# Sums of weight blocks taken in quarters, probabilities scaled by ScalarE in late chunks, and the first odd weight tiles in the ring

## The chip, the cores and the metric

The kernel runs on one core of a Trainium2 chip. A core has a matrix engine (TensorE, in the profile PE, with its weight loads as PEld), a vector engine (VectorE, DVE), a scalar engine (ScalarE, ACT), GpSimd (POOL) and SyncE (SP), which here only issues transfers; ACT issues transfers too. Each of these engines works through its own list of instructions in order and waits for the others by semaphores. SBUF is the working memory, 128 partitions wide; PE writes its sums to PSUM, from where ACT or DVE take them.

The metric is the device time of one execution in microseconds, as the median of several runs. A profile is one further execution, recorded by the hardware.

## The reference

Two layers in one launch: attention with a band and a few global columns, and after it a feed-forward layer on its output.

```python
batch, n_heads, seq, head_dim = (4, 8, 768, 64);  n_global, n_local = (8, 96)
scores = scale * np.matmul(q, k.transpose(0, 1, 3, 2)) + bias     # bias: -slope of the head * distance
scores = np.where(is_global | is_local, scores, -1e9)
a = np.exp(scores - max); a = a / (np.sum(a, axis=-1, keepdims=True) + 1e-09)
attn = np.matmul(a, v)
x = attn.transpose(0, 2, 1, 3).reshape(3072, 512)                 # 3072 tokens
h = x @ w_in                                                      # 512 -> 2048
out = np.maximum(0.01 * h, h) @ w_out                             # 2048 -> 512
```

All arithmetic stands for float32, and the weights arrive as 64-bit floats. The kernel keeps each factor of a product as a high part, rounded to the matrix engine's format (`fp32r`), and a low part, the rest; a product is three matmuls (high by high, low by high, high by low).

## The kernel before, in words

**Tokens.** The 3072 tokens are 24 steps of 128 (`NSTEP`), put together into 11 chunks of 3, 3 and nine times 2 steps (`CHUNKS`). The feed-forward layer has 16 blocks `f` of 128 hidden columns (`NF`), or 8 pairs `p` of two blocks (`NP`); in a pair, `e` is the even and `o` the odd block.

**Attention.** Each step has two units of four heads, 48 in all. `event(t)` does a slice of three units at once: probabilities by values for unit t−2 (`attn_v`, PE), scores for unit t (`scores`, PE), and for unit t then, on DVE, four bias sums with their minimum (`biased`, L215), on ACT four exponentials with their sums (`exps`, L228), and `sums`: two small DVE instructions give the reciprocal `rs` (L249, L250). From unit 14 on (`BY_DVE`) four DVE instructions then multiply the probabilities by it (L256), one DVE instruction transposes them in blocks (L259), and `move` sends them through DRAM into the layout that `attn_v` needs: one transfer out and four back, on SP. The output of `attn_v` is copied by ACT (`keep_x`, L339) and split into high and low by POOL.

**The first two chunks** go through the ordinary loops `ffn1` and `ffn2` (up to about 203 us), while the weights are converted and kept in SBUF: `wout` whole, `win` as 16 tiles. The eight odd tiles of `win` lie in pool `odd` and are also written to DRAM (`wd`), for that pool is given up afterwards.

**The stage of pairs** takes the other nine chunks, 8 pairs each, as 72 steps `s` (`NS`). In a step, in the order of the source:

- the attention events that are due (`ev_pair`): four to a chunk, in its steps 0, 1, 3 and 5;
- `hidden_pair(s)`: 24 matmuls of 256 columns (L478) give the two hidden blocks of a pair, into a PSUM tile `ps_h` in even steps and into the first half of `bank[0]` (`ps_p`) in odd ones. The odd block's weights come by `fetch` from DRAM into a ring of two tiles, two steps ahead, on ACT's queue (L466);
- `gates(s)`: ACT copies the block to `t` (L489), DVE applies the leaky rectifier (L492) and, for a pair by seven products, four small sums of gate blocks (L495); ACT rounds to `gh` (L499), DVE takes the rest `gl` (L500);
- `out_pair(s - 2)`: the matmuls of two steps earlier into the output banks (L527). An ordinary pair takes 12 matmuls of 512 columns, a pair by seven products (a two by two block product with seven block products) 21 of 256. The second half of the tile `bank[0]` is an output bank. `SEVEN` says, chunk by chunk, how many of the eight pairs go by seven products: the last ones, and in the chunk these come last. At a chunk's end `results` gathers the banks into rows in pool `ev` (three buffers) and sends them out;
- in some steps `prepare(p)`: for seven products, `wout` of a pair needs four sums of blocks, each again as high and low. It is done once per pair, as one burst: 12 DVE sums (L508) and 4 ACT casts (L584), with three buffers of `ev` as scratch. There are seven bursts, in steps 10, 12, 14, 18, 20, 26 and 28. The last of the four sums overwrites a block of `wout` that the ordinary form of the pair needs, so it comes only when the pair's ordinary outputs are done.

**The order of the work.** PE's order is that of the source throughout. The other engines' order is that of the source (`pin`) only up to the middle of the second loop; in the stage of pairs a planner sets it before the run: it goes through the source with estimated durations, and each engine takes, of what is ready by these estimates, what stands first in the source. On the chip the engines then keep that order, whatever the real durations are.

**Memory.** Pools are stacked. At step 1, `later.close()` gives up `ffn`, `kept_rows`, `x0` and `odd`, and the pools `ring`, `a` (`gh`, `gl`), `ev` and `w` (the sums `h`, `l`) take the room. A new pool waits for all use of each old pool that it lies over. `a` lies over `kept_rows`, which holds the last output rows of chunk 0 until they are sent (L434, L442). For this reason `gates(0)` and `gates(1)` both stand behind `hidden_pair(1)`.

Of the kernel before, what the change touches and what calls it, by code (L numbers as in the profile page):

```python
# [18 lines left out]
P = 128  # L19
# [12 lines left out]
PAIR = 2  # L32
SEVEN = [0, 3, 5] + [7] * 6
RING = 2
# [18 lines left out]
def fast_path(ctx, tc, qp, kp, vp, wi, wo, nvec, nmall, out, B, H, S):  # L53
# [12 lines left out]
    keep = ctx.enter_context(tc.tile_pool(name="weights", bufs=1))  # L66
    wout = keep.tile([P, NF, 2, DM], F32R, name="wout")
    win = {f: keep.tile([P, 2, NK, P], F32R, tag=f"win{f}", name="win") for f in range(0, NF, 2)}

    const = ctx.enter_context(tc.tile_pool(name="const", bufs=1))  # L70
# [4 lines left out]
    kept_rows = later.enter_context(tc.tile_pool(name="kept_rows", bufs=1))  # L75
    xts = {0: later.enter_context(tc.tile_pool(name="x0", bufs=1))}
    odd = later.enter_context(tc.tile_pool(name="odd", bufs=1))
    nc.gpsimd.memset(odd.tile([P, 16], F32, tag="gap", name="gap"), 0.0)
    win.update({f: odd.tile([P, 2, NK, P], F32R, tag=f"win{f}", name="win") for f in range(1, NF, 2)})
    wd = ctx.enter_context(tc.tile_pool(name="wd", bufs=1, space=bass.MemoryType.DRAM)).tile(  # L80
# [164 lines left out]
    def sums(u):  # L245
        d = units[u]
        sm = d.pop("sm")
        rs = att.tile([P, 16], F32, name="rs")[:, :4]
        pin(nc.vector.tensor_scalar(out=rs, in0=sm, scalar1=1e-9, scalar2=None, op0=ALU.add))  # L249
        pin(nc.vector.reciprocal(out=rs, in_=rs))  # L250
        if u >= BY_DVE:
            pr = d.pop("pr")
            for a in range(2):
                for j in range(2):
                    p, n = head(u, pr, a, j), 2 * a + j
                    pin(nc.vector.tensor_scalar(out=p, in0=p, scalar1=rs[:, n:n + 1], scalar2=1.0, op0=ALU.mult,  # L256
                                                op1=ALU.mult))
            p = blocks(u, pr).rearrange("p c j x -> p (c j x)")
            pin(nc.vector.transpose(out=p, in_=p))  # L259
            move(u, pr)  # L260
            return

        dg = kept_rows.tile([P, 4, HALF], F32, name="dg")
        pin(nc.gpsimd.tensor_tensor(out=dg, in0=eye.unsqueeze(1).to_broadcast([P, 4, HALF]),
                                    in1=rs.unsqueeze(2).to_broadcast([P, 4, HALF]), op=ALU.mult))
        d["dg"] = dg

    def warm(times):
# [191 lines left out]
    def fetch(s):  # L460

        if s >= NS:
            return
        p = at(s)[1]
        streamed[s] = late["ring"].tile([P, 2, NK, P], F32R, name="ring")
        nc.scalar.dma_start(out=streamed[s].rearrange("p a k x -> p (a k x)").bitcast(F32), in_=wd[p])  # L466
# [14 lines left out]

    def gates(s):

        c, p = at(s)
        ps = pair[s]
        n = 8 if fast(c, p) else 4
        t = late["t"].tile([P, 8, P], F32, name="t")
        g = t[:, :4].rearrange("p a b -> p (a b)")
        pin(nc.scalar.copy(out=g, in_=ps))  # L489
        if s >= RING:  # L490
            fetch(s + RING)
        pin(nc.vector.scalar_tensor_tensor(out=g, in0=g, scalar=0.01, in1=g, op0=ALU.mult, op1=ALU.max))  # L492
        if n == 8:
            for o, x, y, op in ((4, 2, 0, ALU.add), (6, 1, 0, ALU.subtract), (5, 4, 1, ALU.subtract), (7, 3, 5, ALU.subtract)):
                pin(nc.vector.tensor_tensor(out=t[:, o], in0=t[:, x], in1=t[:, y], op=op))  # L495
        a0 = n // 8
        gh = late["a"].tile([P, 7, P], F32R, name="gh")
        gl = late["a"].tile([P, 7, P], F32R, name="gl")
        pin(nc.scalar.copy(out=gh[:, :n - a0], in_=t[:, a0:n]))  # L499
        pin(nc.vector.tensor_tensor(out=gl[:, :n - a0], in0=t[:, a0:n], in1=gh[:, :n - a0].bitcast(F32), op=ALU.subtract))  # L500
        pair[s] = gh, gl, a0

# [66 lines left out]

    def prepare(p):  # L570

        e, o = 2 * p, 2 * p + 1
        first = p == NP - 1
        h = late["w"].tile([P, (4 if first else 3) * GT], F32R, tag=f"h{p}", name=f"h{p}")
        l = late["w"].tile([P, 3 * GT], F32R, tag=f"l{p}", name=f"l{p}")
        sides[p] = h, l
        x = [y[:, n] for y in (late["ev"].tile([P, 2, GT], F32, tag="ev", name="wk") for _ in range(3)) for n in range(2)]

        def whole(to, f, n):
            bh, bl = block(f, n)  # L580
            add(to, bh.bitcast(F32), bl.bitcast(F32))

        def split(v, dh, dl):
            pin(nc.scalar.copy(out=dh, in_=v))  # L584
            add(dl, v, dh.bitcast(F32), ALU.subtract)
        cols = [slice(n * GT, (n + 1) * GT) for n in range(4)]
        whole(x[0], e, 1)
        whole(x[1], e, 0)
        add(x[2], x[0], x[1], ALU.subtract)
        split(x[2], h[:, cols[0]], l[:, cols[0]])  # L590
        whole(x[1], o, 1)
        add(x[3], x[1], x[0], ALU.subtract)
        split(x[3], h[:, cols[3 if first else 2]], l[:, cols[2]])
        add(x[0], x[1], x[2], ALU.subtract)
        split(x[0], h[:, cols[1]], l[:, cols[1]])
        whole(x[4], o, 0)
        add(x[5], x[4], x[0], ALU.subtract)
        split(x[5], *block(e, 1))
        if first:
            pin(nc.vector.memset(x[4], 0.0))  # L600
            pin(nc.scalar.copy(out=h[:, cols[2]], in_=x[4]))


# [59 lines left out]
    bank.append(bank[0][:, 1])  # L663
    prepare_at = {}
    for c in range(STD, NCHUNK - 1):
        new = range(NP - 1 - SEVEN[c - STD], NP - 1 - SEVEN[c - STD + 1], -1)
        prepare_at.update({(c - STD + 1) * NP + 2 + 2 * n: p for n, p in enumerate(new)})
    for s in range(NS + 2):
# [4 lines left out]
        if s == 0:  # L673
            ffn2(len(order) - 1)
        elif s == 1:
            later.close()
            for name, n in (("gap0", 1), ("ring", RING), ("gap1", 1), ("a", 2), ("ev", 3), ("w", 1), ):
                late[name] = ctx.enter_context(tc.tile_pool(name=name, bufs=n))
                if name[:3] == "gap":
                    nc.gpsimd.memset(late[name].tile([P, 16], F32, name="gap"), 0.0)  # L680
            for n in range(RING):
                fetch(RING + n)
            gap = late["w"].tile([P, 16], F32, tag="gap", name="gap")
            nc.gpsimd.memset(gap, 0.0)
            gates(0)
            gates(1)
        elif s < NS:
            gates(s)
        if s >= 2:
            out_pair(s - 2)  # L690
        if s in prepare_at:
            prepare(prepare_at[s])

# [341 lines left out]
```

## Time and profile before

| | us |
|---|---|
| median of 3 runs | 676.23 (675.62 to 677.06) |
| the profiled execution | 672.49 |
| its span, first to last instruction | 670.7 |
| PE busy | 624.4 (93%) |
| DVE busy | 471.1 (70%) |
| ACT busy | 305.6 (46%) |

Instruction rows of a timeline show the start, the length, the engine and line, what is written and read, how many, and in brackets the idle time of the engine before it with what ended it. `PEld` are weight loads, `SPq` and `ACTq` transfers at their issue. Rows of groups show the busy time, the mean in ns and the idle time before them. The granted clock is that of PE, 1.00 at full speed. Some matmul rows are missing from a trace, and the ends of matmuls are modelled.

### The profile page before, as it was taken

Reading aid. Unit: us, or ns where it says so; the run is one execution under the profiler, and the core shown is the slowest. Engines: PE = TensorE matmul, PEld = TensorE weight load, DVE = VectorE, ACT = ScalarE, POOL = GpSimd, SP = SyncE. Lnnn points to the kernel's source line nnn. Section 1 sums busy time; section 2 is a strip of 40 time slices with the busy share of each in tenths; the row PEclk is TensorE's granted clock in tenths of the full one; section 3 lists DMA queues with packets and bytes.
Section 4 is the critical chain, followed back from the end, with each engine's and each line's share of the span. In section 5 each row is a group of like instructions: output and inputs, shape, how many; then the busy total and the mean of one; then the engine's idle time right before and its main releaser. Section 6 shows DMA issues by size and latency. Waiting matters only on the chain.

```text
span 670.7 us, 16703 instructions
## 1 busy us (share of the span) xinstructions
PE 624.4 (93%) x6509; PEld 570.8 (85%) x6509; DVE 471.1 (70%) x1362; ACT 305.6 (46%) x786; POOL 89.2 (13%) x151
## 2 busy tenths in 40 slices
PE   5579999999998999899799969999999999999994
PEld 4468889998886888789689969999999999999993
DVE  5979988886645436966776687776876766854644
ACT  5977755555442324434434334533544443422331
POOL 3435600000110101001010010110120020010000
PEclk9999999999998999899999979999999999999998
DMA  7785644423557657455645726575775664632311
GB/s 287 268 285 188 205 157 157 157 95 110 173 172 260 195 161 235 135 174 186 207 158 174 244 108 213 168 247 166 240 228 192 222 220 158 207 124 95 126 64 37
DMA packets 63334, 120.71 MB, mean 180 GB/s; under 512 B 8976, under 2 KB 28432, under 8 KB 63248
## 3 DMA queue, kind: packets, MB, share of 16 engines
q1 hardware_dynamic: 53168, 82.86, 38.2%
q10 hardware_dynamic: 10080, 36.70, 16.7%
q8 instruction: 53, 0.87, 0.6%
q14 instruction: 33, 0.27, 0.1%
HBM read 96.21 MB, written 23.33 MB: 178 GB/s over the span
## 4 chain that ended last, share of the span: by engine, by line
PE 73%; DVE 8%; DMA 8%; ACT 5%; issue 2%; POOL 2%; SPq 1%; ACTq 0%; DVEq 0%; POOLq 0%
PE ps_m L527 18%; PE ps_h L478 13%; PE ps_p L478 12%; PE ps_p L527 7%; PE ps_av L333 4%; ACT pr L228 3%; PE ps_av L201 3%; PE ps_h L944 3%; PE ps_h L946 3%; PE ps_o L965 3%; PE ps_h L945 3%; PE ps_o L964 3%; PE ps_o L966 3%; DMA vr<-in_vp_dram 2%; DMA kr<-in_kp_dram 2%
## 5 line engine op out<-in xcount | busy, mean ns | idle before, releaser
L499 ACT CAST gh<-t 128x896 fp32r<-128x896 f32 (+1 forms) x72 | 60.6, 843 | 138.0 <-DVE t L495 54.1
L500 DVE TENSOR_TENSOR gl<-t,gh 128x896 fp32r<-128x896 f32 (+1 forms) x72 | 70.0, 973 | 59.4 <-ACT gh L499 59.2
L228 ACT ACTIVATE pr<-pr,nmall 128x192 f32<-128x192 f32 (+1 forms) x192 | 83.3, 436 | 22.8 <-DVE nmall L215 22.8
L527 PE MATMUL ps_m<-wout,gh 128*128 128x256 f32 (+1 forms) x388 | 88.6, 310 | 3.0 <-ACT gh L499 3.0
L49 POOL TENSOR_SCALAR xh<-x 128x256 fp32r<-128x256 f32 x48 | 27.5, 572 | 462.5 <-ACT x L339 380.1
L492 DVE SCALAR_TENSOR_TENSOR t<-t 128x512 f32<-128x512 f32 x72 | 49.5, 687 | 35.4 <-ACT t L489 35.4
L527 PEld LDWEIGHTS ps_m<-wout,gh 128*128 128x128 f32 x388 | 61.7, 190 | 5.4 <-ACT gh L499 3.2
L527 PE MATMUL ps_p<-wout,gh 128*128 128x256 f32 (+1 forms) x188 | 50.6, 352 | 12.5 <-ACT t L489 12.4
L527 PE MATMUL ps_m<-wout,gl 128*128 128x256 f32 (+1 forms) x194 | 60.8, 313 | 0.0
L478 PE MATMUL ps_p<-xh,win 128*128 128x256 f32 x296 | 59.8, 287 | 0.0
L478 PE MATMUL ps_h<-xh,win 128*128 128x256 f32 x296 | 59.8, 287 | 0.0
L478 PE MATMUL ps_h<-xh,ring 128*128 128x256 f32 x280 | 55.0, 282 | 0.0
L478 PE MATMUL ps_p<-xh,ring 128*128 128x256 f32 x280 | 54.0, 278 | 0.0
L478 PEld LDWEIGHTS ps_p<-xh,win 128*128 128x128 f32 x296 | 47.7, 188 | 6.0 <-issue 5.7
L215 DVE CUSTOM_DVE_ANT_0 pr<-ps_av,nbw 128x192 f32<-128x192 f32 x136 | 40.4, 352 | 17.3 <-ACT x L339 17.3
L495 DVE TENSOR_TENSOR t<-t 128x128 f32<-128x128 f32 x200 | 49.6, 285 | 2.5
L478 PEld LDWEIGHTS ps_h<-xh,win 128*128 128x128 f32 x296 | 49.1, 194 | 2.5 <-issue 2.2
L527 PEld LDWEIGHTS ps_p<-wout,gh 128*128 128x128 f32 x188 | 32.7, 196 | 19.8 <-ACT t L489 16.1
L478 PEld LDWEIGHTS ps_h<-xh,ring 128*128 128x128 f32 x280 | 46.0, 192 | 0.0
L478 PEld LDWEIGHTS ps_p<-xh,ring 128*128 128x128 f32 x280 | 45.0, 188 | 0.0
L944 PE MATMUL ps_h<-xh,win 128*128 128x384 f32 x128 | 44.4, 347 | 0.5 <-ACT win L720 0.5
L527 PE MATMUL ps_m<-h,gh 128*128 128x256 f32 (+1 forms) x150 | 43.9, 293 | 0.0
(135 smaller groups left out, 1607.4 us busy)
## 6 DMA issues: line engine op xcount, KB each, us to landing
ring<-wd ACTq DMA_DIRECT2D x70, 512.0 KB, 3.4
via<-pr SPq DMA_DIRECT2D x30, 384.0 KB, 2.6
pt_d<-via SPq DMA_DIRECT2D x120, 96.0 KB, 3.4
kr<-in_kp_dram SPq DMA_DIRECT2D x40, 256.0 KB, 3.9
vr<-in_vp_dram SPq DMA_DIRECT2D x40, 256.0 KB, 3.7
wst<-in_wi_dram SPq DMA_DIRECT2D x16, 512.0 KB, 3.7
wst<-in_wo_dram SPq DMA_DIRECT2D x16, 512.0 KB, 3.9
qs<-in_qp_dram SPq DMA_DIRECT2D x24, 256.0 KB, 4.5
```

What stands on the lines that cost most here:

```text
L49: return eng.tensor_scalar(out=dst, in0=src, scalar1=1.0, scalar2=1.0, op0=ALU.mult, op1=ALU.mult)
L201: tc.keep_in_program_order(nc.tensor.matmul(own(u, av[qf, j, a * KW:(a + 1) * KW]), lhsT=q[rows, a, qf], rhs=keys(rows, a, f), start=True, ...
L215: pin(nc.vector.tensor_tensor_reduce(out=head(u, pr, a, j), in0=own(u, ps[:, j, a * KW:(a + 1) * KW]), in1=nb, scale=-0.125, scalar=3.0e38 ...
L228: pin(nc.scalar.activation(out=p, in_=p, func=AF.Exp, scale=-1.0, bias=nm[:, 2 * a + j:2 * a + j + 1], accum_out=sm[:, 2 * a + j:2 * a + j ...
L333: tc.keep_in_program_order(nc.tensor.matmul(av[out, a, cols], lhsT=v[rows, t, j, :], rhs=near(rows, j, t, fs), start=(n == 0), stop=(n == ...
L478: tc.keep_in_program_order(nc.tensor.matmul(o, lhsT=w[:, y, k], rhs=x[:, k, :], start=(k + i == 0), stop=(k == NK - 1 and i == 2)))
L492: pin(nc.vector.scalar_tensor_tensor(out=g, in0=g, scalar=0.01, in1=g, op0=ALU.mult, op1=ALU.max))
L495: pin(nc.vector.tensor_tensor(out=t[:, o], in0=t[:, x], in1=t[:, y], op=op))
L499: pin(nc.scalar.copy(out=gh[:, :n - a0], in_=t[:, a0:n]))
L500: pin(nc.vector.tensor_tensor(out=gl[:, :n - a0], in0=t[:, a0:n], in1=gh[:, :n - a0].bitcast(F32), op=ALU.subtract))
L527: tc.keep_in_program_order(nc.tensor.matmul(to, lhsT=x[:, a], rhs=y, start=first and n == 0, stop=last and n == 2))
L944: tc.keep_in_program_order(nc.tensor.matmul(ps, lhsT=w[:, 0, k], rhs=xh[:, k, :CT], start=(k == 0), stop=False))
```

## The change

- `SEVEN` becomes `[0, 4, 7, 7, ...]`: 53 pairs go by seven products, before 50.
- The ring is a pool of its own, laid out at the start. Its two tiles first hold `win[1]` and `win[3]`; `odd` holds the other six. `x0` and `odd` change places. `later.close()` comes at step 0, after the last `ffn2`, and `gates` runs in each step, from step 0 on, each with its `fetch`.
- `prepare(p, part)` does one of the four sums of a pair: two sums of high and low, their sum or difference, the cast, the rest. Where a burst kept sums as scratch, a part forms them again from high and low. The three sums of a part and its cast stand in `gates` between the rounding of the gates and their rest, the part's own rest after that. Two parts stand in each of steps 2 to 7 (the first three of pairs 7 to 4), one in each of steps 8 to 23.
- Once pool `a` exists, that is from step 1 on, the probabilities are multiplied by four ACT instructions, no longer by DVE. The transposing and the transfers (`turn`) stand behind `gates` from step 1 on.

The diff, without the removed body of `prepare`:

```diff
-SEVEN = [0, 3, 5] + [7] * 6
+SEVEN = [0, 4] + [7] * 7
...
-    wout = keep.tile([P, NF, 2, DM], F32R, name="wout")
     win = {f: keep.tile([P, 2, NK, P], F32R, tag=f"win{f}", name="win") for f in range(0, NF, 2)}
+    ring = ctx.enter_context(tc.tile_pool(name="ring", bufs=RING))
+    win.update({2 * n + 1: ring.tile([P, 2, NK, P], F32R, name="ring") for n in range(RING)})
+    outer = ctx.enter_context(tc.tile_pool(name="outer", bufs=1))
+    wout = outer.tile([P, NF, 2, DM], F32R, name="wout")
...
-    xts = {0: later.enter_context(tc.tile_pool(name="x0", bufs=1))}
     odd = later.enter_context(tc.tile_pool(name="odd", bufs=1))
     nc.gpsimd.memset(odd.tile([P, 16], F32, tag="gap", name="gap"), 0.0)
-    win.update({f: odd.tile([P, 2, NK, P], F32R, tag=f"win{f}", name="win") for f in range(1, NF, 2)})
+    win.update({f: odd.tile([P, 2, NK, P], F32R, tag=f"win{f}", name="win") for f in range(2 * RING + 1, NF, 2)})
+    xts = {0: later.enter_context(tc.tile_pool(name="x0", bufs=1))}
+    nc.gpsimd.memset(xts[0].tile([P, 16], F32, tag="gap", name="gap"), 0.0)
...
         if u >= BY_DVE:
-            pr = d.pop("pr")
+            pr = d["pr"]
             for a in range(2):
                 for j in range(2):
                     p, n = head(u, pr, a, j), 2 * a + j
-                    pin(nc.vector.tensor_scalar(out=p, in0=p, scalar1=rs[:, n:n + 1], scalar2=1.0, op0=ALU.mult,
-                                                op1=ALU.mult))
-            p = blocks(u, pr).rearrange("p c j x -> p (c j x)")
-            pin(nc.vector.transpose(out=p, in_=p))
-            move(u, pr)
+                    if late.get("a"):
+                        pin(nc.scalar.activation(out=p, in_=p, func=AF.Copy, scale=rs[:, n:n + 1]))
+                    else:
+                        pin(nc.vector.tensor_scalar(out=p, in0=p, scalar1=rs[:, n:n + 1], scalar2=1.0, op0=ALU.mult,
+                                                    op1=ALU.mult))
+            if not late.get("a"):
+                turn(u)
             return
...
+    def turn(u):
+
+        pr = units[u].pop("pr")
+        p = blocks(u, pr).rearrange("p c j x -> p (c j x)")
+        pin(nc.vector.transpose(out=p, in_=p))
+        move(u, pr)
...
-    def gates(s):
+    def gates(s, sums=()):
...
-        if s >= RING:
-            fetch(s + RING)
+        fetch(s + RING)
...
         pin(nc.scalar.copy(out=gh[:, :n - a0], in_=t[:, a0:n]))
+        rest = [prepare(p, part) for p, part in sums]
         pin(nc.vector.tensor_tensor(out=gl[:, :n - a0], in0=t[:, a0:n], in1=gh[:, :n - a0].bitcast(F32), op=ALU.subtract))
+        for low in rest:
+            low()
...
-    def prepare(p):
+    def prepare(p, part):
 
         e, o = 2 * p, 2 * p + 1
         first = p == NP - 1
+        if part == 0:
+            h = late["w"].tile([P, (4 if first else 3) * GT], F32R, tag=f"h{p}", name=f"h{p}")
+            l = late["w"].tile([P, 3 * GT], F32R, tag=f"l{p}", name=f"l{p}")
+            sides[p] = h, l
+        h, l = sides[p]
+        x, y = (late["ev"].tile([P, 2, GT], F32, tag="ev", name="wk")[:, n] for n in range(2))
+        t1, t3, t2 = ((h[:, i * GT:(i + 1) * GT], l[:, j * GT:(j + 1) * GT]) for j, i in ((0, 0), (2, 3 if first else 2), (1, 1)))
+        (ah, al), (bh, bl), (dh, dl) = ((block(e, 1), block(e, 0), t1), (block(o, 1), block(e, 1), t3), (block(o, 1), t1, t2),
+                                        (block(o, 0), t2, block(e, 1)))[part]
+        add(x, ah.bitcast(F32), al.bitcast(F32))
+        add(y, bh.bitcast(F32), bl.bitcast(F32))
+        add(x, x, y, ALU.subtract)
+        pin(nc.scalar.copy(out=dh, in_=x))
+        if first and part == 0:
+            pin(nc.vector.memset(y, 0.0))
+            pin(nc.scalar.copy(out=h[:, 2 * GT:3 * GT], in_=y))
+        return lambda: add(dl, x, dh.bitcast(F32), ALU.subtract)
...
-    prepare_at = {}
-    for c in range(STD, NCHUNK - 1):
-        new = range(NP - 1 - SEVEN[c - STD], NP - 1 - SEVEN[c - STD + 1], -1)
-        prepare_at.update({(c - STD + 1) * NP + 2 + 2 * n: p for n, p in enumerate(new)})
+    three = [(p, n) for p in (7, 6, 5, 4) for n in range(3)]
+    sums_at = {2 + n: three[2 * n:2 * n + 2] for n in range(6)}
+    sums_at.update({NP + n: [x] for n, x in enumerate(
+        [(3, 0), (3, 1), (7, 3), (6, 3), (5, 3), (4, 3), (3, 2), (3, 3)] + [(p, n) for p in (2, 1) for n in range(4)])})
...
-        elif s == 1:
             later.close()
-            for name, n in (("gap0", 1), ("ring", RING), ("gap1", 1), ("a", 2), ("ev", 3), ("w", 1), ):
+            for name, n in (("a", 2), ("ev", 3), ("w", 1)):
                 late[name] = ctx.enter_context(tc.tile_pool(name=name, bufs=n))
-                if name[:3] == "gap":
-                    nc.gpsimd.memset(late[name].tile([P, 16], F32, name="gap"), 0.0)
-            for n in range(RING):
-                fetch(RING + n)
-            gap = late["w"].tile([P, 16], F32, tag="gap", name="gap")
-            nc.gpsimd.memset(gap, 0.0)
-            gates(0)
-            gates(1)
-        elif s < NS:
-            gates(s)
+            nc.gpsimd.memset(late["w"].tile([P, 16], F32, tag="gap", name="gap"), 0.0)
+        if s < NS:
+            gates(s, sums_at.get(s, ()))
+        for t in ev_pair.get(s, ()):
+            if s and t < NUNIT:
+                turn(t)
         if s >= 2:
             out_pair(s - 2)
-        if s in prepare_at:
-            prepare(prepare_at[s])
```

More of the change, by code (lines that the diff above doesn't have):

```diff
@@ L464, in fetch @@
         p = at(s)[1]
-        streamed[s] = late["ring"].tile([P, 2, NK, P], F32R, name="ring")
+        streamed[s] = ring.tile([P, 2, NK, P], F32R, name="ring")
         nc.scalar.dma_start(out=streamed[s].rearrange("p a k x -> p (a k x)").bitcast(F32), in_=wd[p])
@@ L568, in results @@
             nc.sync.dma_start(out=out[r0:r0 + P, :], in_=rows[n])
-    def prepare(p):
+    def prepare(p, part):
         e, o = 2 * p, 2 * p + 1
         first = p == NP - 1
[L574 to L601, printed above, removed]
```

## The prediction

> **What bounds the kernel now.** I began with the page, at the engine rows.
>
> ```profile
> span 670.7 us, 16703 instructions
> PE 624.4 (93%) x6509; PEld 570.8 (85%) x6509; DVE 471.1 (70%) x1362; ACT 305.6 (46%) x786; POOL 89.2 (13%) x151
> ```
>
> PE is the bound by far, so I asked where it is not at full work. The stage of pairs begins near 203; cut into stretches of about a chunk (columns: window, length, PE busy, granted clock, DMA share, GB/s) it shows two kinds of chunk:
>
> ```profile
> 373.00:425.00 52.00, 46.54 (x460) 0.93 0.56 179
> 425.00:474.00 49.00, 49.00 (x534) 1.00 0.63 202
> ```
>
> From 425 on PE is never idle and never slow; nothing but fewer matmuls can gain there. The time to be had lies between 203 and 425. PE's waits, grouped, and the four long ones in the timeline:
>
> ```profile
> PE ps_p L527 <- ACT t L489: 12.4, 6, 5.3
> PE ps_m L527 <- ACT gh L499: 3.0, 1, 3.0
> ...
> 212.92 0.73 PE L527 MATMUL ps_m<-wout,gh 128*128 128x512 f32 x2 [3.03 <-ACT gh L499]
> ...
> 277.61 0.73 PE L527 MATMUL ps_p<-wout,gh 128*128 128x512 f32 x2 [2.44 <-ACT t L489]
> ...
> 333.18 1.22 PE L527 MATMUL ps_p<-wout,gh 128*128 128x512 f32 x2 [3.95 <-ACT t L489]
> ...
> 391.93 0.79 PE L527 MATMUL ps_p<-wout,gh 128*128 128x256 f32 x2 [5.27 <-ACT t L489]
> ```
>
> The last three stand in the steps of `prepare`. The engines' timelines there show a chain: a DVE sum waits for a buffer of pool `ev` that an output transfer still reads; the ACT cast of that sum waits for DVE; the copy `t<-ps_p` stands behind it in ACT's order; and PE does not go on in the second half of that PSUM tile before the copy has read the first.
>
> ```profile
> 386.57 0.42 DVE L508 TENSOR_TENSOR wk<-wk 128x256 f32<-128x256 f32 x1 [4.48 <-DMA out_dram<-part]
> ...
> 387.03 0.40 ACT L584 CAST h<-wk 128x256 fp32r<-128x256 f32 x1 [3.91 <-DVE wk L508]
> ...
> 391.32 0.56 ACT L489 COPY t<-ps_p 128x512 f32<-128x512 f32 x1
> ```
>
> Each long wait is followed by a slow clock (columns: window, length, busy time of PE, PEld, DVE, ACT, POOL, then clock, DMA share, GB/s):
>
> ```profile
> 207.00:220.00 13.00, 9.97 (x93) 7.96 (x92) 5.75 (x13) 3.65 (x9) 0.29 (x2) 0.87 0.80 268
> 275.00:285.00 10.00, 7.55 (x38) 6.54 (x38) 8.40 (x32) 4.70 (x16) 0.00 (x0) 0.83 0.29 91
> 331.00:340.00 9.00, 6.82 (x35) 6.02 (x36) 7.94 (x27) 2.90 (x12) 0.00 (x0) 0.81 0.27 104
> 386.00:397.00 11.00, 5.73 (x29) 5.53 (x28) 10.40 (x35) 4.43 (x15) 2.03 (x2) 0.73 0.21 75
> ```
>
> Length times (1 − clock) is what each costs: 1.7, 1.7, 1.7 and 3.0, in all 8.1 us. So 15.4 of waits and 8.1 of slow clock lie in this stage.
>
> **The change, part by part.** *Quarters of sums.* 28 quarters take the place of seven bursts. A quarter has four DVE instructions (three sums and a rest) where a burst had twelve in all, so there are 28 more, at the 0.42 us of the sum above 11.8 us of DVE. They sit where DVE waits for the rounded gates, take one buffer of `ev` each, not three at once, and during the first chunk no output uses that pool. I take the chain above to be gone: 12.4 us of waits and 1.7 + 1.7 + 3.0 = 6.4 of clock.
>
> Is there room on DVE? Two quarters a step, in steps 2 to 7, are 8 × 0.42 = 3.4 us. The gate takes 0.69, its rest has the same size, an event four bias sums, two small ones of 0.18 and the transposes:
>
> ```profile
> L492 DVE SCALAR_TENSOR_TENSOR t<-t 128x512 f32<-128x512 f32 x72 | 49.5, 687 | 35.4 <-ACT t L489 35.4
> L215 DVE CUSTOM_DVE_ANT_0 pr<-ps_av,nbw 128x192 f32<-128x192 f32 x136 | 40.4, 352 | 17.3 <-ACT x L339 17.3
> ...
> 432.10 0.97 DVE L259 STREAM_TRANSPOSE pr<-pr 128x768 f32<-128x768 f32 x1
> ...
> 223.20 0.73 PE L527 MATMUL ps_p<-wout,gh 128*128 128x512 f32 x2 [0.32 <-ACT t L489]
> ...
> 425.83 0.83 PE ps_av L333 x32
> ...
> 430.34 1.76 PE ps_m L527 x15
> 432.11 0.35 PE ps_p L527 x3
> ...
> 432.81 2.74 PE ps_h L478 x24
> 435.55 0.69 PE ps_m L527 x3
> ```
>
> So DVE has 4.8 us in a step without an event, which PE fills for 2.74 + 4 × 0.695 = 5.5; and 4.8 + 1.4 + 0.4 + 1.0 = 7.6 in a step with one (3 and 5), against some 7.3 of PE (425.83 to 432.81 is such a step, with products by seven, 0.3 shorter). There is no slack in these two, and the quarters' lag runs into the next step. The cost of that shows in odd steps with an event and ordinary outputs (3, 5, 9, 11, 13): they wait 0.32 for the copy already (the row of 223.20), and a late bias sum makes the exponentials, and behind them the copy, later. From nothing to 1.5 us each, the length of a whole quarter; I take 0.5, near the row: 2.5. Results of chunks 0 and 1 share `ev` with the quarters: 0 to 2 us (a transfer's time, less what covers it), I take 1.0 for both together.
>
> *Three more pairs by seven products.* From 430.34 to 432.81 such outputs take 2.47, ordinary ones four times 0.695, 2.78. 50 pairs become 53: 3 × 0.31 = 0.9 us. The four gate sums of each go to DVE, which after step 23 has less to do than before.
>
> *Ring first.* Gates 0 no longer stand behind the second hidden block. But pool `a` still lies over `kept_rows`, and its first cast waits until the last output has left those rows:
>
> ```profile
> 202.83 1.19 ACTq L466 DMA_DIRECT2D ring<-wd  x2
> ...
> 205.57 0.35 SPq L442 DMA_DIRECT2D out_dram<-kept  x1
> ...
> 212.25 0.62 ACT L499 CAST gh<-t 128x512 fp32r<-128x512 f32 x1 [4.31 <-DMA out_dram<-kept]
> ...
> 208.00:210.00 2.00, 1.88 (x17) 1.69 (x15) 2.00 (x6) 0.00 (x0) 0.00 (x0) 1.00 1.00 390
> ```
>
> Those 6.7 us from issue to landing pass with the DMA engines full (share 1.00). The two ring loads issued together at 202.83 will go one near 201, behind the first copy `t`, and one near 207; so 512 KB, 1.3 us at 390 GB/s, are out of that output's way, and something of its neighbours' too. I let it land near 210.2; the cast ends at 210.9 and PE, ready at 212.92 − 3.03 = 209.9, waits 1.0. Bounds: nothing, or the whole 3.03 with its 1.7 of clock.
>
> [...]
>
> *Scaling on ACT.* 29 units, four instructions each, leave DVE for ACT. Transposes and the unit's five SP transfers go behind the gates, at most 1.5 us later; their reader comes two events on, three steps or some 17 us, and the transfers take
>
> ```profile
> via<-pr SPq DMA_DIRECT2D x30, 384.0 KB, 2.6
> pt_d<-via SPq DMA_DIRECT2D x120, 96.0 KB, 3.4
> ```
>
> so this costs nothing, nor what stands behind them on SP, loads for two events ahead. ACT's price for four: at least four casts at half of the 0.71 that a pair of 128x256 took, 1.4 us; at most four exponentials at 445 ns, 1.8. I take 1.4, as neither reads an accumulator. ACT, at 46%, has the time. What matters is the place, for behind the scaling stands the gates' copy:
>
> ```profile
> 341.27 0.71 ACT L584 CAST h<-wk 128x256 fp32r<-128x256 f32 x2
> L228 ACT ACTIVATE pr<-pr,nmall 128x192 f32<-128x192 f32 x48 | 21.3, 445 | 8.6 <-DVE nmall L215 8.6
> ...
> 430.36 0.18 DVE L250 RECIPROCAL rs<-rs 128x4 f32<-128x4 f32 x1
> 430.38 0.59 ACT L489 COPY t<-ps_p 128x512 f32<-128x512 f32 x1 [0.26 <-PE ps_p L478]
> ...
> 443.58 0.56 ACT L489 COPY t<-ps_p 128x512 f32<-128x512 f32 x1
> 443.91 0.18 DVE L250 RECIPROCAL rs<-rs 128x4 f32<-128x4 f32 x1
> ...
> 444.54 0.34 PE ps_p L527 x3
> ```
>
> The copy starts with the reciprocal or before it, and the scaling needs that one's result. A planner that takes what is ready puts the copy first. Then the cost is nothing.
>
> *Sum*, against the profiled execution: 12.4 + 6.4 for the bursts, 3.0 + 1.7 − 1.0 at the start, 0.9 for products make 23.4 off; 2.5 + 1.0 come back: 19.9. That execution took 672.5 (the span and 1.8 around it), the median of the runs shown is 676.2, 3.7 more; the gain taken from each gives 652.6 and **656.3**.
>
> **The rivals.** *All waits go*, also the 4.5 that I left in: 651.8. For it speaks the stretch 425 to 474, where DVE has results, an event and sums in one step and PE never waits; against it the count of 7.6 to 7.3.
>
> *The waits move.* The start keeps its 3.03 and 1.7, which is 3.7 more than I left there, and one step of chunk 0 to 2 still collides, as ACT casts of quarters stand before the copy: 2.4 to 4 and 1.7 of clock. 664 to 666. For it: ACT takes its work in order, and where the planner put the first cast, it stood for 4.31 us. Against it: one quarter at a time, not four.
>
> *The scaling goes ahead of the copy*, the slower side. Scaling from 430.54 on would end at 431.9 to 432.3, the copy at 432.5 to 432.9, and PE wants it at 432.11: 0.4 to 0.8. In the step of 443.58 it would end at 446.0 to 446.5, and PE wants it at 444.54: 1.5 to 2.0. The third odd event of a chunk I put between these, as an estimate 0.7 to 1.2. That is 2.6 to 4.0 a chunk, in six chunks 16 to 24; chunks 0 and 1, whose ordinary outputs want the tile 1.06 earlier, lose 10 to 12 in five steps. 26 to 36 us, against 24.4 to be gained at most, give 678 to 688. It decides from about 1 us a step on. Against it: at 443.58 the copy comes before any reciprocal.
>
> *It doesn't do what it says*: the planner may draw the quarters forward into one burst, since nothing but buffers holds them; waits come back, and 676 with them.
>
> **How the numbers follow.** Forecast 0.58 (653 to 660), all waits gone 0.13, waits moved 0.20, no effect 0.03, scaling ahead 0.06. A measurement of this kernel can tell about 0.2%, 1.35 us, from no change. Faster: 0.58 + 0.13 + 0.20 = 0.91; same 0.03; slower 0.06. The range goes from 650.5, all waits gone with a microsecond of scatter, to 668, waits moved with one more slow clock.
>
> **What would show it.** Clock 1.00 from 225 to 425 and no PE wait above 1.5 us there; before it one wait near 1 us at the first `ps_m`; no DVE sum waiting for `out_dram<-part`; at odd events ACT's order exponentials, copy `t`, scaling. The opposite order, with waits at `ps_p` in every chunk up to 620, proves me wrong, as does a new slow clock, or a full chunk after 425 that takes more than 49 us.

## The result, and the profile after

The changed kernel takes 665.52 us (median of 4 runs, 663.10 to 667.69) where the kernel before takes 675.92 (672.47 to 677.06): a ratio of 0.9854, 95% interval 0.9804 to 0.9903. The forecast was 656.3 us, 19.9 off; 10.4 came.

The page's engine rows of the kernel after (busy us, share of the span, instructions):

```profile
span 663.8 us, 16802 instructions
PE 620.7 (94%) x6536; PEld 569.5 (86%) x6536; DVE 458.2 (69%) x1286; ACT 348.1 (52%) x902; POOL 89.9 (14%) x150
```

PE is still the bound, ACT has taken on 42 us of scaling, and DVE is down by 13. The span is not the best measure here, because the time before the stage of pairs scatters (below). The first matmul of that stage in the timeline of before:

```profile
197.68 0.39 PE L478 MATMUL ps_h<-xh,win 128*128 128x256 f32 x1
```

and in that of after:

```profile
200.57 0.38 PE L491 MATMUL ps_h<-xh,win 128*128 128x256 f32 x1
```

From there to the end it is 670.7 − 197.68 = 473.0 us before and 663.8 − 200.57 = 463.2 after: 9.8 less. This **stage time** is used from here on. Where the long waits stood, after (windows: length, busy time of the engines, clock, DMA share, GB/s):

```profile
207.00:220.00 13.00, 10.75 (x112) 9.04 (x108) 10.13 (x30) 7.38 (x21) 1.15 (x2) 1.00 0.88 279
275.00:285.00 10.00, 6.10 (x28) 4.83 (x27) 8.78 (x29) 5.20 (x18) 1.24 (x2) 0.84 0.36 123
336.00:343.00 7.00, 5.51 (x26) 5.52 (x27) 6.14 (x19) 3.54 (x12) 0.00 (x0) 0.52 0.33 116
373.00:417.00 44.00, 44.00 (x469) 41.77 (x468) 29.98 (x90) 24.08 (x62) 5.59 (x8) 1.00 0.69 223
```

The stretch from 373 to 417 holds the place of the third burst: PE is never idle there now. But two stretches look as before, idle PE and half clock behind it. PE's waits in the timeline after:

```profile
213.91 0.51 PE L542 MATMUL ps_m<-wout,gl 128*128 128x512 f32 x1 [0.47 <-DVE gl L513]
218.15 1.26 PE L346 MATMUL ps_av<-pt_d,vr 64*64 64x128 f32 x24 [1.65 <-DMA pt_d<-via]
...
238.66 0.73 PE L542 MATMUL ps_p<-wout,gh 128*128 128x512 f32 x2 [1.31 <-ACT t L502]
281.23 0.83 PE L542 MATMUL ps_p<-wout,gh 128*128 128x512 f32 x2 [3.90 <-ACT t L502]
337.49 0.79 PE L542 MATMUL ps_p<-wout,gh 128*128 128x256 f32 x2 [3.72 <-ACT t L502]
```

Ahead of 281.23, DVE and ACT show the chain that the prediction called gone:

```profile
270.98 0.42 DVE L523 TENSOR_TENSOR wk<-h,l 128x256 f32<-128x256 f32 x1 [2.39 <-DMA out_dram<-part]
...
278.10 0.41 ACT L601 CAST wout<-wk 128x256 fp32r<-128x256 f32 x1 [1.72 <-DVE wk L523]
...
280.59 0.58 ACT L502 COPY t<-ps_p 128x512 f32<-128x512 f32 x1
```

A sum waits for a buffer of `ev` that an output transfer reads, casts of sums wait for DVE, the copy stands behind them. How can that be, with one quarter a step? It isn't one quarter a step. The sums' instructions by stretch (line L523 alone; up to 300 these are quarters only, as the results of chunk 0 need no sums):

```profile
217.00:230.00 13.00, 8.20 (x23) 1.00 0.60 203
230.00:243.00 13.00, 9.21 (x26) 1.00 0.57 175
243.00:257.00 14.00, 0.42 (x1) 1.00 0.54 165
257.00:270.00 13.00, 0.41 (x1) 1.00 0.75 230
270.00:286.00 16.00, 9.64 (x25) 0.89 0.50 164
```

The 26 us to 243 have 49, the next 27 us two, the 16 us behind those 25; each quarter makes four of them. Nothing in the written order holds a quarter in its step, so the planner issues each as soon as its inputs and a buffer are there: chunk 0's are all done by 243, those of the steps from 10 on run in a row once the results' buffers come free. The bursts are still there, two of three.

### The profile page after: what moved, and what is told of

It reads as the page before. It is cut to its first block, busy times and chain, and to the rows that moved or that the text cites. A ratio compares the mean times of both kernels' runs of the same rounds, so it can differ in the third digit from the quotient of the medians.

```text
span 663.8 us, 16802 instructions
## 1 busy us (share of the span) xinstructions
PE 620.7 (94%) x6536; PEld 569.5 (86%) x6536; DVE 458.2 (69%) x1286; ACT 348.1 (52%) x902; POOL 89.9 (14%) x150
## 4 chain that ended last, share of the span: by engine, by line
PE 75%; DVE 11%; ACT 5%; DMA 4%; issue 2%; POOL 1%; SPq 0%; ACTq 0%; DVEq 0%; POOLq 0%
PE ps_m L542 19%; PE ps_h L491 13%; PE ps_p L491 13%; PE ps_p L542 6%; PE ps_av L346 4%; PE ps_av L205 3%; ACT pr L232 3%; PE ps_h L940 3%; PE ps_h L942 3%; PE ps_o L960 3%; PE ps_o L961 3%; PE ps_h L941 3%; PE ps_o L962 3%; DVE wk L523 3%; DMA out_dram<-part 1%
## 5 line engine op out<-in xcount | busy, mean ns | idle before, releaser
L542 PE MATMUL ps_m<-wout,gh 128*128 128x256 f32 (+1 forms) x394 | 86.9, 302 | 0.0
L491 PE MATMUL ps_p<-xh,win 128*128 128x256 f32 x288 | 58.2, 287 | 0.0
L491 PE MATMUL ps_h<-xh,win 128*128 128x256 f32 x288 | 58.1, 286 | 0.0
L491 PE MATMUL ps_h<-xh,ring 128*128 128x256 f32 x288 | 56.4, 281 | 0.0
L542 PE MATMUL ps_p<-wout,gh 128*128 128x256 f32 (+1 forms) x182 | 46.3, 336 | 10.3 <-ACT t L502 10.2
L507 DVE TENSOR_TENSOR t<-t 128x128 f32<-128x128 f32 x212 | 52.0, 285 | 2.7
L491 PEld LDWEIGHTS ps_p<-xh,win 128*128 128x128 f32 x288 | 46.3, 188 | 5.9 <-issue 5.7
L542 PE MATMUL ps_m<-h,gh 128*128 128x256 f32 (+1 forms) x159 | 46.1, 290 | 0.0
L261 ACT ACTIVATE pr<-pr,rs 128x192 f32<-128x192 f32 (+1 forms) x116 | 42.5, 438 | 4.0 <-DVE rs L254 3.0
L542 PEld LDWEIGHTS ps_p<-wout,gh 128*128 128x128 f32 x182 | 30.4, 191 | 16.4 <-ACT t L502 13.5
```

The source lines that it names most:

```text
L261: pin(nc.scalar.activation(out=p, in_=p, func=AF.Copy, scale=rs[:, n:n + 1]))
L491: tc.keep_in_program_order(nc.tensor.matmul(o, lhsT=w[:, y, k], rhs=x[:, k, :], start=(k + i == 0), stop=(k == NK - 1 and i == 2)))
L542: tc.keep_in_program_order(nc.tensor.matmul(to, lhsT=x[:, a], rhs=y, start=first and n == 0, stop=last and n == 2))
```

## The experiments

All change the kernel after unless said otherwise; ratios are to the kernel before, run on the same chip. Its medians on the chips used lie between 674.28 and 676.05 us, so medians of different experiments can be set side by side to a microsecond or two.

**Quarters held with their gates** (`held`): everything that `gates` issues in a step with quarters keeps its place in the written order.

```diff
+            pinned[0] = s in sums_at
             gates(s, sums_at.get(s, ()))
+            pinned[0] = False
```

> The changed kernel, but the gates of the steps that hold quarters (2 to 23) keep the order of the source on DVE and ACT, so that the planner can't draw quarters of later steps forward. Theory A (the two long waits that are left, 3.90 and 3.72 us with 1.7 and 3.4 us of slow clock, come from quarters drawn together behind an output transfer): both waits and both slow clocks go, some 11 us off the changed kernel's 665.5, 653 to 657. Theory B (DVE has too much work in steps 3 to 21, wherever the quarters stand): the waits only spread, 662 to 668. Theory C (the scaling on ACT makes the copies late): no change, 664 to 667.

Measured: 672.2 us (667.56 to 676.52), ratio 0.996 (0.993 to 0.9991), slower than all three theories had it. The quarters stay in their steps and no DVE sum waits for an output, but PE waits in eight odd steps, 1.45 to 2.45 us each. Step 9, on ACT and then on PE:

```profile
270.03 1.49 ACT L261 ACTIVATE pr<-pr,rs 128x192 f32<-128x192 f32 x4 [0.51 <-DVE rs L254]
271.43 0.56 ACT L502 COPY t<-ps_p 128x512 f32<-128x512 f32 x1
...
272.04 0.73 PE L542 MATMUL ps_p<-wout,gh 128*128 128x512 f32 x2 [2.45 <-ACT t L502]
```

Held gates stand behind all that is written ahead of them, the event's scaling too, so the scaling goes ahead of the copy. That confounds the test: it says nothing of the bursts, but it prices the prediction's slower rival.

**Scaling on DVE again** (`dve_scale`), `turn` left where the change puts it.

```diff
-                    if late.get("a"):
-                        pin(nc.scalar.activation(out=p, in_=p, func=AF.Copy, scale=rs[:, n:n + 1]))
-                    else:
-                        pin(nc.vector.tensor_scalar(...))
+                    pin(nc.vector.tensor_scalar(...))
```

> The changed kernel with the probabilities scaled by DVE again in all chunks, transposes and transfers still behind the gates. Theories A and B: DVE has 1.0 us more in each event, which counts only where DVE is short, in steps 3 to 21: 0 to 3 us slower than the changed kernel, 665 to 669, and the same stretch times after step 26. Theory C: faster by 3 to 10 us, 656 to 662.

Measured: 663.82 us (662.68 to 667.07), ratio 0.9838 (0.9793 to 0.9883), not to be told from the kernel after. With the bursts in place the scaling on ACT is worth nothing that shows.

**No sums at all** (`no_sums`): the quarters are left out, and the products multiply `block(o, 0)` in place of the sums, so the output isn't the reference's.

```diff
-            gates(s, sums_at.get(s, ()))
+            gates(s)
```

> The changed kernel without any sums of weight blocks: the products that need them take a block of the second matrix as it is, so the output is not the reference's; PE's work is the same. Theories A and B: the waits from step 3 on and their slow clocks go, 10.2 + 5.1 us, some 650 us; this is the floor of what any placing of the sums can give. Theory C: the waits stay, above 660.

Measured: 650.01 us (648.23 to 650.84), ratio 0.9618 (0.9563 to 0.9672). PE waits only at 215.81 and 217.71, for the probabilities. So some 15 us of the kernel after belong to the sums.

**Rows of chunks 2 and 3 not sent out** (`no_out`): the output lacks them; the sums are all there.

```diff
-        for n in range(PAIR):
+        for n in range(PAIR if c > STD + 1 else 0):
```

> The changed kernel without sending out the rows of chunks 2 and 3 (their output is left out), so that no sum can wait for an output transfer of these chunks; the quarters' order is the planner's. If the transfer alone makes the two long waits: both go, 653 to 656. If the drawing together alone does: 664 to 667. Theory A takes both: the waits shrink to 1 to 2 us each and keep at most one slow clock, 657 to 661.

Measured: 656.47 us (655.85 to 658.39), ratio 0.9719 (0.9664 to 0.9774). PE's two long waits become these, in the timeline:

```profile
280.12 0.74 PE L542 MATMUL ps_p<-wout,gh 128*128 128x512 f32 x2 [1.51 <-ACT t L502]
...
331.29 0.50 PE L542 MATMUL ps_p<-wout,gh 128*128 128x256 f32 x2 [0.30 <-ACT t L502]
```

A burst alone costs 1.5 us at most; that its buffers wait for transfers makes the rest, by medians 9 us in all.

**Only the quarters held** (`held_q`): the three DVE additions of a quarter keep their place, gates, copies, casts and scaling stay free.

```diff
+        pinned[0] = True
         add(x, ah.bitcast(F32), al.bitcast(F32))
         add(y, bh.bitcast(F32), bl.bitcast(F32))
         add(x, x, y, ALU.subtract)
+        pinned[0] = False
```

> Only the three DVE additions of each quarter are bound to their place in the written order; gates, copies and scaling stay free, so the copy of an odd step goes ahead of the scaling. Theory A (the planner draws the quarters forward into a burst, whose scratch then waits for an output transfer, and that makes the waits of 3.90 and 3.72 us and the half clock behind them): both waits fall below 1.5 us, no stretch of half clock is left after 230 us, 653 to 658 us. Theory B (a quarter that shares its scratch with the results stalls wherever it stands, and the odd steps are short of DVE time anyway): waits of 2 to 4 us come back at other steps behind the results of chunks 0 and 1, 662 to 668 us.

Measured: 654.08 us (652.40 to 656.31), ratio 0.9693 (0.9666 to 0.972), 11.4 us below the kernel after and the best version that computes the reference. PE's waits, grouped (total, times, longest):

```profile
PE ps_av L346 <- DMA pt_d<-via: 2.2, 1, 2.2
PE ps_p L542 <- ACT part L573: 1.1, 1, 1.1
PE ps_p L542 <- ACT t L502: 1.1, 2, 0.6
PE ps_m L542 <- ACT gh L511: 0.3, 1, 0.3
```

The wait for `part` stands behind the results of chunk 1, whose copies go on ACT behind a quarter's cast. The stretch of the first long wait, by engines:

```profile
275.00:285.00 10.00, 9.96 (x62) 8.33 (x61) 5.67 (x18) 4.54 (x15) 0.36 (x1) 1.00 0.68 198
```

The sums by stretch, which are spread now:

```profile
230.00:243.00 13.00, 5.95 (x16) 1.00 0.63 192
243.00:257.00 14.00, 6.55 (x18) 1.00 0.50 149
257.00:270.00 13.00, 3.17 (x8) 1.00 0.60 172
270.00:286.00 16.00, 4.42 (x11) 1.00 0.81 259
```

Its stage starts here in the timeline:

```profile
199.97 0.38 PE L491 MATMUL ps_h<-xh,win 128*128 128x256 f32 x1
```

It takes 652.4 − 199.97 = 452.4 us, 20.6 less than before. The theory of the quarters drawn forward holds.

**Event of step 1 as before** (`held_early`): as `held_q`, with scaling on ACT and the late `turn` from step 2 on only.

```diff
-            if s and t < NUNIT:
+            if s > 1 and t < NUNIT:
                 turn(t)
+        late["scale"] = s > 0
```

(`sums` asks `late.get("scale")` in place of `late.get("a")`.)

> As held_q, and the event of step 1 scales its probabilities on DVE and sends them at once, ahead of the gates, as the kernel before does; ACT scales from step 2 on. Theory A for the start (the wait of 1.65 us for the probabilities comes from their scaling and transpose standing behind the first rounding, which waits for the transfer of the kept rows): no wait for the probabilities near 218 us, 1.5 to 3 us less than held_q. Theory B (the probabilities' transfers are slow because the ring's transfers run beside them): the wait stays within 0.5 us of held_q's, and so does the time.

Measured: 654.23 us (652.12 to 656.35), ratio 0.9697 (0.9668 to 0.9726): nothing gained. The probabilities that PE waits for are not those of step 1 but of step 0. In the timeline they go out to `via` at 206.37 and are fetched back from 210.61 on, and PE still waits:

```profile
206.37 0.40 SPq L243 DMA_DIRECT2D via<-pr  x1
...
210.61 1.75 SPq L245 DMA_DIRECT2D pt_d<-via  x4
...
216.60 0.40 PE L346 MATMUL ps_av<-pt_d,vr 64*64 64x128 f32 x2 [1.40 <-DMA pt_d<-via]
```

**No quarter behind the results** (`held_skip`): as `held_early`, steps 10, 11, 18 and 19 without quarters.

```diff
+    sums_at.update({8: [(3, 0), (3, 1)], 9: [(3, 2), (2, 0)], 12: [(7, 3)], 13: [(6, 3)], 14: [(5, 3)], 15: [(4, 3)],
+                    16: [(3, 3), (2, 1)], 17: [(2, 2)]})
+    sums_at.update({20 + n: [x] for n, x in enumerate([(2, 3), (1, 0), (1, 1), (1, 2), (1, 3)])})
```

> As held_early, and no quarter stands in the steps behind the results of chunks 0 and 1 (steps 10, 11, 18 and 19); the steps 8, 9 and 16 take two. Theory A: what is left of waits at those steps goes, 0 to 3 us less than held_early, 650 to 656 us. Theory B: the transfers of results last longer than two steps, so that the wait moves to step 12 or 20 (over 1.5 us there), and the time stays within 1 us of held_early's.

Measured: 655.26 us (653.26 to 655.60), ratio 0.9701 (0.9673 to 0.9729). The small waits sit elsewhere (1.08 at 265.53, in a step that has two quarters now, 1.01 at 317.57, 1.31 at 323.38), the time is the same. One quarter a step was fine.

**The new start alone** (`start_only`), on the kernel before: new places of the tiles, gates and fetches from step 0; the bursts, the older list of pairs and scaling on DVE stay. The diff shows what it takes back of the change.

```diff
-SEVEN = [0, 4] + [7] * 7
+SEVEN = [0, 3, 5] + [7] * 6
...
-            gates(s, sums_at.get(s, ()))
+            gates(s)
...
+        if s in prepare_at:
+            prepare(prepare_at[s])
```

> The kernel before with the new start alone: first two odd tiles in the ring, gates, copies and fetches in every step from step 0. Pair sums in bursts behind steps 10, 12 and so on, the older list of seven-product pairs, and scaling on DVE stay as before. Theory A (the start is worth what the forecast gave it: 3.0 + 1.7 - 1.0): 3.7 us less than before, 670.5 to 672.5 us beside a before of 675, the bursts' waits of 2.4, 4 and 4 to 5 us unchanged. Theory B (the removed wait hid that of the probabilities of step 0, which shows now): a wait of 1 to 2.2 us for the probabilities near 218 us stays, and the gain is 0.5 to 2 us, 673 to 675 us.

Measured: 673.29 us (670.97 to 675.59), ratio 0.9961 (0.9942 to 0.9981). PE's first waits in the timeline:

```profile
213.14 0.73 PE L535 MATMUL ps_m<-wout,gh 128*128 128x512 f32 x2 [0.29 <-ACT gh L507]
218.02 0.40 PE L342 MATMUL ps_av<-pt_d,vr 64*64 64x128 f32 x2 [1.58 <-DMA pt_d<-via]
219.50 0.73 PE L342 MATMUL ps_av<-pt_d,vr 64*64 64x128 f32 x22 [1.07 <-DMA pt_d<-via]
```

The 3.03 us for the rounded gates are gone, and behind them the probabilities are late, by 2.65 in two pieces. All in all these waits come to 0.29 + 2.65 = 2.9, so they account for next to none of the gain of some 2.7 us. Most of it lies in the later chunks, as the next experiment shows.

**The places of the tiles alone** (`layout_only`): as `start_only`, with pools, gates and fetches at step 1 as before.

```diff
-        fetch(s + RING)
+        if s >= RING:
+            fetch(s + RING)
...
+        if s == 1:
+            for n in range(RING):
+                fetch(RING + n)
+            gates(0)
+            gates(1)
+        elif 1 < s < NS:
+            gates(s)
```

> The kernel before with the new places of the tiles alone: the ring is laid out at the start and holds the first two odd tiles, the output weights lie behind it; pools, gates, copies and fetches of the first steps come at step 1 as before. Theory A (the places of the tiles make the matmuls of the seven-product pairs slightly faster): the groups of product matmuls that write ps_m take 277 to 278 ns, not 280 to 281, the last full chunk takes 48.7 us, not 49.3, and the time is 1.5 to 4 us less than before. Theory B (the earlier order of the first gates and fetches makes it): 280 to 281 ns, 49.3 us, and the time within 1.3 us of before.

Measured: 672.9 us (669.51 to 674.77), ratio 0.9977 (0.9952 to 1.0002). A group of product matmuls from 470 to 640 (count, busy, mean ns, idle before), in the kernel before:

```profile
L527 PE MATMUL ps_m<-wout,gh 128*128 128x256 f32 x150 | 29.7, 280 | 0.0
```

and in this one:

```profile
L536 PE MATMUL ps_m<-wout,gh 128*128 128x256 f32 x150 | 29.4, 277 | 0.0
```

The matmuls are shorter, as the first theory has it, and the chunks of eight steps from the fifth on, counted between first hidden matmuls, shrink from 48.1, 49.2 and 49.3 us to 47.8, 48.8 and 48.7. The total is smaller than that theory's 1.5 to 4 us, 1.4 by medians, and its interval just takes in no change. What about the places does it, wasn't tried. By stage time the two are alike: 670.7 − 200.94 = 469.8 us here and 670.0 − 200.65 = 469.4 in `start_only`.

PE's wait for the first rounding is gone here too (0.17 us in the timeline, at 213.31), though gates and fetches come at step 1 as before. So the earlier gates aren't needed for that. With the ring laid out at the start its second load goes out only at 212.65, no longer ahead of the kept rows, and the last of these takes 3.7 us from its issue at 208.93 to the cast at 212.64, where the kernel before has 6.7. That fits the prediction's reason, ring loads out of the rows' way; the reason wasn't tested by itself.

**The kernel before once more** (`before_again`).

> The kernel before, profiled a second time, for its lead-in alone: in its first profile the first matmul of the stage of pairs starts at 197.68 us and no stretch of half clock lies before 45 us; in the five other profiles it starts at 199.4 to 200.8 us with 7 to 14 us of half clock there. If that is scatter of the execution, this profile may start at 199 to 201 us as well, with such stretches; if it is a cost of the new place of the tiles, it starts at 197.5 to 198 us again.

Its timeline:

```profile
198.89 0.38 PE L478 MATMUL ps_h<-xh,win 128*128 128x256 f32 x1
...
214.47 0.73 PE L527 MATMUL ps_m<-wout,gh 128*128 128x512 f32 x2 [3.38 <-ACT gh L499]
219.18 0.72 PE L333 MATMUL ps_av<-pt_d,vr 64*64 64x128 f32 x21 [1.03 <-DMA pt_d<-via]
```

The stage starts at 198.89, just short of the 199 forecast for scatter, with half clock around 25 to 32 and 42 to 45; it takes 671.1 − 198.89 = 472.2 us. So the start of the stage scatters by over a microsecond with one and the same kernel. Both executions profiled, 672.49 and 672.91 us, are also faster than this kernel's medians. The twelve profiles with the new places start the stage at 199.15 to 201.24; whether a part of that is a cost of the places stays open.

**Kept rows not sent** (`no_kept`): `held_q`, whose output lacks the three rows of chunk 0.

```diff
+            if c == 0:
+                continue
             r0 = (first_step[c] + tt) * P
             nc.sync.dma_start(out=out[r0:r0 + P, :], in_=ob)
```

> As held_q, but the three rows of chunk 0 that are added up around 204 us are not sent out, so the output lacks them. Theory A (the wait of 2.17 us for the probabilities of step 0 comes from their transfers sharing the DMA engines with these rows): it falls below 1 us, and the wait for the first rounding (0.34 us) goes, 1.5 to 4 us less than held_q. Theory B (their own two hops and the loads of queries, keys and ring tiles make it): it stays above 1.5 us and the time stays within 1 us of held_q's.

Measured: 653.27 us (652.88 to 655.98), ratio 0.968 (0.9643 to 0.9717). The wait for the probabilities falls from 2.17 to 0.41 + 1.00, the one for the first rounding is gone; the time falls by 0.8, which can't be told from nothing. These rows are a part of the cause, not all of it; the other part is left open.

**Held quarters, scaling on DVE** (`held_dve`): the edit of `dve_scale` on `held_q`.

> As held_q, with the scaling on DVE in every step, so that gates, quarters and scaling share DVE. Theory A (with the quarters in their steps the scaling on ACT is worth something, since an odd step has 0.9 to 1.0 us of scaling and 1.4 to 2.8 us of quarters on DVE ahead of its gate or its rest): waits of 0.5 to 2 us at the odd event steps of chunks 0 and 1, 1 to 5 us more than held_q. Theory B (DVE has room for both): within 0.7 us of held_q.

Measured: 657.51 us (657.02 to 659.25), ratio 0.974 (0.9713 to 0.9767), 3.4 above `held_q`; the stage takes 655.2 − 200.2 = 455.0 us, 2.5 more. PE's wait behind the results grows from 1.07 to 2.67, in the timeline:

```profile
323.08 0.74 PE L539 MATMUL ps_p<-wout,gh 128*128 128x512 f32 x2 [2.67 <-ACT part L570]
```

It stands at the results, not at odd event steps as expected. The same edit that was worth nothing with bursts is worth some 3 us without them.

## Why the prediction was right and where it was wrong

The time fell inside the range, with half of the forecast gain. That is no merit of the forecast's own sum: the range reached so far because of the rival "the waits move", priced at 664 to 666, and 665.5 lies there by luck. Of that rival's two parts one came, casts of quarters ahead of the copy, with two long waits and not one; the other, a start that keeps its 3.03 us, did not.

Term by term, in the stage:

| term | forecast, us off | after | held_q |
|---|---|---|---|
| long waits of the bursts | 11.7 (12.4 less the small ones) | 11.7 → 7.6: 4.0 | 11.7 |
| their half clock | 6.4 | 6.4 → 5.0: 1.4 | 6.4 |
| start: wait and clock | 3.7 | 2.6 | 0.5 |
| seven products | 0.9 | 0.9 (not measured by itself) | 0.9 |
| odd steps, results | −2.8 (3.5 less the small waits of before) | −1.9 | −1.4 |
| left over | none | 2.8 | 2.5 |
| sum | 19.9 | 9.8 | 20.6 |

The long waits are 2.44 + 3.95 + 5.27 before and 3.90 + 3.72 after. Clock after is 10 × 0.16 + 7 × 0.48. The start is 3.03 + 1.7 against 0.47 + 1.65 after, and against 0.34 + 2.17 and one half-clock stretch of 1.7 in `held_q` (single hidden matmuls there take 0.41 us from 220.87 on, 0.28 from 222.79 on). Eight of the twelve profiles with the new places have such a stretch at the start, among them `held` (clock 0.76 from 217 to 224); that the profile of after has none (1.00 from 207 to 220) is luck, and 1.7 of its 2.6 with it. Odd steps are what they wait beyond the 0.7 that the small waits took before (0.32, 0.20 and 0.19): 0.56 at 224, 1.31 at 239 and 0.75 at 353 after; 0.44, 0.61 and 1.07 in `held_q`. What is left over goes with the shorter product matmuls of the new places, 0.3 to 0.6 a full chunk; as `layout_only` as a whole showed 1.4 us by medians and 3.2 by stage time, up to half of it may be scatter or small gaps that no row carries.

- **The step that failed** is "I take the chain above to be gone: 12.4 us of waits and … 6.4 of clock". It took the written place of a quarter for its time of issue. The prediction named this ("the planner may draw the quarters forward into one burst, since nothing but buffers holds them") and gave it 0.03, with the whole gain lost. Two bursts of three came back, the third didn't. Of the 18.1 us without the small waits 5.4 came, 12.7 are missing. `held_q` shows that the mechanism was right given the place: there the term comes whole.
- **The start** kept 0.47 where 1.0 was left, and the kept rows do land sooner (3.5 us from the last issue at 208.57 to the cast at 212.03, before 6.7), as forecast; but the removed wait had covered a later one: the probabilities of step 0, in transfers beside the kept rows and the ring. The prediction asked whether their transfers were moved, not whether they had been on time only because PE was late. The rival in which "waits move" has this form, with another place and a smaller price.
- **Odd steps and results**: 2.5 + 1.0 forecast, 2.6 measured with bursts, 2.1 without (the table has what goes beyond the 0.7 of before). The step holds; the size was on the high side.
- **Scaling**: order and place came as forecast, copy first, then scaling. Four of 192 columns take 1.49, not 1.4, and four of 128 take 1.28, in the timeline of after:

```profile
281.13 1.28 ACT L261 ACTIVATE pr<-pr,rs 128x128 f32<-128x128 f32 x4
...
338.17 1.49 ACT L261 ACTIVATE pr<-pr,rs 128x192 f32<-128x192 f32 x4
```

  The rival with the scaling ahead was priced at 0.4 to 2.0 a step in later chunks and 10 to 12 in the five steps of chunks 0 and 1; `held` shows 1.45 to 2.38 in chunk 2, and 1.79 + 1.79 + 2.45 + 1.57 + 1.57 = 9.2 there.
- **What was to show it**: full chunks are no longer than 49 us, as said. Waits above 1.5 us, a DVE sum waiting for `out_dram<-part` and half clock past 225 all appear, each named as a sign against.

## What to carry to other kernels

Where a planner sets the order, the written place of an instruction is not its time: ask what holds it, and if only a buffer does, expect it early and in a heap, and hold it by an order of its own rather than by holding what stands around it. A wait that is taken away can uncover the next late thing on the same engine (here 3.03 us for the rounded gates went to 0.47, and 1.65 for the probabilities came); look for what lands during the wait. Test parts of a change again once the main fault is mended: scaling on ACT was worth nothing with bursts and 3 us without.

## What the runs showed of the hardware

In these traces the half clock doesn't follow the length of a gap. In the profile of the kernel before taken again, a gap of 3.38 us ended at 214.47 (its row above), and the clock behind it stayed at 1.00 (windows: length, busy time of the engines, clock, DMA share, GB/s):

```profile
213.00:220.00 7.00, 4.50 (x49) 3.11 (x53) 2.68 (x4) 2.35 (x4) 0.00 (x0) 1.00 0.78 238
```

In the timeline of `held` stand two gaps of the same 1.79 us:

```profile
227.19 0.73 PE L542 MATMUL ps_p<-wout,gh 128*128 128x512 f32 x2 [1.79 <-ACT t L502]
241.91 0.73 PE L542 MATMUL ps_p<-wout,gh 128*128 128x512 f32 x2 [1.79 <-ACT t L502]
```

The clock behind them differs, by its windows:

```profile
225.00:232.00 7.00, 5.21 (x35) 4.44 (x34) 5.01 (x11) 3.29 (x8) 0.00 (x0) 1.00 0.51 170
241.00:248.00 7.00, 6.09 (x29) 5.39 (x30) 5.11 (x11) 2.08 (x6) 0.00 (x0) 0.76 0.56 181
```

The second costs 7 × 0.24 = 1.7 us of clock, one stretch of 3.4 at half. In the kernel before the stretches of half clock that start between 203 and 425 us last 3.4 us (from 213.59, 278.45 and 333.06) and 6.8 (from 391.09), in the one after 3.4 (from 281.72) and 6.8 (from 336.33). In the 3.41 us ahead of each, at full clock, PE was busy for 0.96 us at most; before:

```profile
210.18:213.59 3.41, 0.67 (x2) 0.30 (x2) 0.93 (x3) 1.14 (x2) 0.00 (x0) 1.00 0.98 334
275.04:278.45 3.41, 0.96 (x5) 0.71 (x5) 3.38 (x20) 3.04 (x12) 0.00 (x0) 1.00 0.26 56
329.65:333.06 3.41, 0.00 (x0) 0.00 (x0) 3.41 (x16) 2.88 (x12) 1.00 (x2) 1.00 0.13 45
387.68:391.09 3.41, 0.00 (x0) 0.00 (x0) 3.41 (x10) 0.96 (x4) 2.03 (x2) 1.00 0.01 2
```

and after:

```profile
278.31:281.72 3.41, 0.49 (x2) 0.45 (x3) 3.35 (x17) 3.27 (x13) 0.00 (x0) 1.00 0.02 4
332.92:336.33 3.41, 0.84 (x8) 0.64 (x6) 3.41 (x13) 1.69 (x7) 1.82 (x2) 1.00 0.20 72
```

With the two gaps in `held` PE was busy for 1.82 us and, ahead of the half clock, for 1.63:

```profile
225.60:229.01 3.41, 1.82 (x8) 1.53 (x9) 2.28 (x5) 1.53 (x5) 0.00 (x0) 1.00 0.65 215
239.25:242.67 3.42, 1.63 (x8) 1.07 (x7) 1.60 (x4) 2.04 (x6) 0.00 (x0) 1.00 0.86 275
```

The gap of 3.38 us, which no half clock followed, lies in these two stretches, with 1.52 and 1.93:

```profile
209.57:212.99 3.42, 1.52 (x14) 1.32 (x12) 2.05 (x5) 0.00 (x0) 0.00 (x0) 1.00 1.03 394
212.99:216.40 3.41, 1.93 (x7) 1.33 (x8) 1.89 (x3) 1.73 (x3) 0.00 (x0) 1.00 0.88 275
```

So 1.63 us of busy time stood ahead of half clock and 1.52 ahead of full. What decides between the two is not shown by these runs.

And the places of tiles in SBUF are worth something by themselves: the same matmuls take 277 ns in one layout and 280 in the other, 0.3 to 0.6 us in a chunk of seven-product pairs. The other profiles bear it out: 277 or 278 in all twelve with the new places (277 in after and `start_only`), 280 in both of the old.
